# Weighting expert 0's output one expert later, with expert 1 added at a ratio, in an attention-and-experts kernel

## The chip, the cores and the metric

The kernel runs on one core of a Trainium2 chip. The metric is the device time of one execution in microseconds (us), the median over several executions. All executions quoted here were of the fast state, and their granted TensorE clock was 0.986 to 1.0 of full speed. A profile shows a span of its own, about 2 us shorter than the time of the same execution (696.4 us in a run of 698.21 us). Engine names in the profile: PE is TensorE, PEld its weight load, DVE is VectorE, ACT is ScalarE, POOL is GpSimd. SBUF is the core's working memory; PSUM is the memory that PE writes its products to, here in banks that are used again and again.

## The reference

Attention for 4 batches and 8 heads (768 tokens, head size 64), then a mixture of 8 experts over the 3072 tokens, each token weighted for each expert by a matrix `P` that Sinkhorn rounds have balanced. Cut to what matters:

```python
x = attention(q, k, v, ...)              # 3072 tokens x 512
P = np.exp(x @ w_gate - max)             # 3072 x 8
for _ in range(8):                       # Sinkhorn: rows, then columns
    P /= P.sum(1, keepdims=True) + 1e-09
    P /= P.sum(0, keepdims=True) + 1e-09
    P *= N / E
for e in range(8):
    h = np.maximum(x @ w1[e], 0.0)
    out += P[:, e:e + 1] * (h @ w2[e])
```

Every output row is a sum over all experts. Expert 0 can be computed before `P` is known if its result is multiplied by `P[:, 0]` later.

## The kernel before

The kernel does that. Expert 0 is computed while attention and the Sinkhorn rounds run, and its unweighted output goes to `acc` in SBUF. Experts 1 to 7 follow, each in six chunks of 512 tokens. Each product of a chunk is built from seven block products instead of eight (Strassen's scheme): PE does 14 layer-1 groups and 7 layer-2 groups a chunk, VectorE makes the sums of blocks, ScalarE copies partial sums out of PSUM. While PE does layer 1 of one chunk, it does layer 2 of the chunk before, in turns.

`Pne` holds the weights; `acc[c]` is the output of chunk `c`. The weighting of expert 0 was a generator that expert 1's loop advanced four times per chunk:

```python
def weight_first(c):
    for nb in range(4 * c, 4 * c + 4):
        nc.scalar.activation(out=acc_of(nb), in_=acc_of(nb), func=AF.Copy,
                             bias=0.0, scale=Pne[:, nb, 0:1])
        yield
...
def copy(g, name, bank):       # layer 1: a partial sum leaves PSUM, VectorE reads it later
    R[name] = mp.tile([128, 2, 256], F32, tag=f"R{name}", bufs=1, name=f"R{name}")
    nc.scalar.activation(out=R[name], in_=banks[g, bank], func=AF.Copy, bias=0.0, scale=1.0)
...
def add(bank, i, n, by_dma):   # layer 2: add weight * result to acc
    ...
        w = Pne[:, 4 * c + 2 * q + i, e:e + 1]
        if by_dma:             # ScalarE weights into t, a DMA with accumulation adds t to acc
            nc.scalar.activation(out=t[:, q, :], in_=banks[bank][q], func=AF.Copy,
                                 bias=0.0, scale=w)
        else:                  # VectorE adds in place
            nc.vector.scalar_tensor_tensor(out=dst, in0=banks[bank][q], scalar=w, in1=dst,
                                           op0=ALU.mult, op1=ALU.add)
...
if e == 1:
    gens["first"] = weight_first(c)
    gens["x"] = combine_x((c + 1) % NCH)
for slot in range(7):
    go("l1", 2 if n == 0 and slot == 0 else 1)
    ...
    go("l2")
    if slot in (2, 3, 5, 6):
        go("first")
...
with tc.manual_schedule(engines={mybir.EngineType.DVE}):
    ...
```

In this part only VectorE's instructions keep the order of the program. The compiler chooses the order of the others, and puts forward what it takes to be ready (the profile and the run e5 below show the order that results).

The softmax here doesn't subtract the row's maximum and nothing guards it: scores larger than these inputs give would overflow.

## Time and profile before

The time was 698.92 us in three runs.

| what | value | view of the profile |
|---|---|---|
| PE busy | 681.5 of 696.4 us | page, part 1 |
| chain that ended last | 89% PE | page, part 4 |
| ScalarE busy, 176 to 203 us | 26.75 of 27.00 us | table of stretches |
| weightings of `acc` | 24, all between 176.2 and 202.4 us | instructions of one source line |
| PE's period, expert 1's six chunks | 13.89, 12.93, 12.32, 12.33, 12.32, 12.22 us | timeline of PE |

A "period" here is the time from one chunk's first layer-2 group to the next chunk's. The steady value is 12.22 us: 14 layer-1 groups of 0.4365 us and 7 layer-2 groups of 0.873 us, one after the other.

The timeline of PE (columns: start, duration, engine, line, operation and operands) gives the starts of the first three chunks' layer 2:

```profile
182.03 1.04 PE L801 MATMUL l2y<-w_1_2286,hT_0_3295 128*128 128x256 f16 x8
...
195.92 1.04 PE L801 MATMUL l2y<-w_1_2286,hT_1_3369 128*128 128x256 f16 x8
...
208.85 1.04 PE L801 MATMUL l2y<-w_1_2286,hT_2_3548 128*128 128x256 f16 x8
```

The differences are 13.89 and 12.93 us. The list of waits (columns: who waited for whom, us in total, times, longest), cut to PE's waits in this stage, names the cause:

```profile
PE l1y L736 <- ACT R_3482 L745: 1.2, 1, 1.2
PE l1y L736 <- ACT R_3663 L745: 0.4, 1, 0.4
```

In this program PE may not write a PSUM bank again before ScalarE has copied it to an R tile. The timelines show the longer of the two waits, on PE and on ScalarE:

```profile
190.24 0.60 PE L736 MATMUL l1y<-T_1_3324,w_1_2284 128*128 128x256 f16 x4
192.00 0.60 PE L736 MATMUL l1y<-T_1_3324,S_1_3308 128*128 128x256 f16 x4 [1.16 <-ACT R_3482 L745]
```

```profile
187.02 2.00 ACT L659 ACTIVATE acc_81<-acc_81,Pne 128x512 f32<-128x512 f32 x3
188.86 1.38 ACT L659 ACTIVATE acc_82<-acc_82,Pne 128x512 f32<-128x512 f32 x2
190.09 0.89 ACT L815 ACTIVATE add<-l2z,Pne 128x256 f32<-128x256 f32 x2
190.80 0.66 ACT L745 ACTIVATE R_3476<-l1w 128x512 f32<-128x512 f32 x1
191.27 0.67 ACT L745 ACTIVATE R_3482<-l1y 128x512 f32<-128x512 f32 x1
```

L659 is the weighting. Five of them stand in front of the `add`, and the copy that PE needs comes behind it. A little earlier ScalarE's timeline shows the same pattern:

```profile
182.66 0.63 ACT L745 ACTIVATE R_3375<-l1y 128x512 f32<-128x512 f32 x1
183.14 1.98 ACT L659 ACTIVATE acc_80<-acc_80,Pne 128x512 f32<-128x512 f32 x3
184.98 0.63 ACT L745 ACTIVATE R_3399<-l1w 128x512 f32<-128x512 f32 x1
```

`acc_80` belongs to chunk 1, although PE is at layer 2 of chunk 0: the compiler had put the weightings of all six chunks as early as it could. The table of stretches (columns: stretch and length; busy time and instruction count of PE, PEld, DVE, ACT, POOL; PE's clock; DMA share; GB/s) shows no idle time on ScalarE:

```profile
176.00:203.00 27.00, 25.84 (x209) 20.13 (x207) 22.69 (x47) 26.75 (x51) 2.63 (x3) 1.00 0.48 80
```

Here ScalarE's 26.75 us is the number to read, and beside it PE's 25.84 us of 27: PE is idle for over a microsecond.

### The profile page before, as it was taken

The page shows a single profiled execution, that of the slowest core. Times are in us where ns is not written, and L with a number is a line of the kernel's source. Part 1 is how long each engine was busy: PE and PEld are TensorE (multiplying, and loading weights), DVE is VectorE, ACT ScalarE, POOL GpSimd, SP SyncE. Part 2 cuts the span into 40 slices and gives each one's busy share as a digit, 9 for nine tenths or more (in the row PEclk, how much of TensorE's full clock was granted, in tenths as well). Part 3 has the DMA queues.
Part 4 walks back from the last instruction along what each step waited for, and adds up shares of the span by engine and source line. Part 5 has one row for each costly group of instructions (what it writes and reads, how often), then busy time and mean ns, then how long its engine had stood idle before and what let it go on. Part 6 is the DMA issues. An engine that isn't in the chain of part 4 may idle for free.

```text
span 696.4 us, 16662 instructions
## 1 busy us (share of the span) xinstructions
PE 681.5 (98%) x6753; PEld 567.3 (81%) x6753; DVE 574.1 (82%) x1149; ACT 420.0 (60%) x775; POOL 167.1 (24%) x201
## 2 busy tenths in 40 slices
PE   7999999999999999999999999999999999999997
PEld 3666666666688888888888888888888888888885
DVE  7886766657889988898898879888898888988785
ACT  6778776764985555546556554655556555555651
POOL 7555430000021131213212221222212212121210
PEclk9999999999999999999999999999999999999999
DMA  9999990001634386437834593359533954245786
GB/s 178 175 172 152 68 80 3 1 2 22 100 61 78 61 135 108 75 64 121 138 57 76 90 152 68 62 81 154 90 58 64 152 103 77 48 76 110 143 158 152
DMA packets 102974, 65.59 MB, mean 94 GB/s; under 512 B 67056, under 2 KB 83440, under 8 KB 102896
## 3 DMA queue, kind: packets, MB, share of 16 engines
q0 software_dynamic: 93696, 57.17, 66.0%
q1 hardware_dynamic: 7552, 6.30, 3.9%
q8 instruction: 53, 0.87, 0.6%
q10 hardware_dynamic: 1648, 1.05, 0.5%
q14 instruction: 25, 0.20, 0.1%
HBM read 52.45 MB, written 6.29 MB: 84 GB/s over the span
## 4 chain that ended last, share of the span: by engine, by line
PE 89%; ACT 5%; DVE 3%; issue 1%; DMA 1%; ACTq 0%; DVEq 0%
PE l1y L736 20%; PE l2y L801 20%; PE l2w L801 10%; PE l1w L736 10%; PE l1z L736 5%; PE l2z L801 5%; PE l1b L716 1%; DMA ret_u<-in_is_retrieval_dram 1%; DVE acc_80 L818 0%; ACT acc_81 L659 0%; ACT acc_82 L659 0%; ACT add L815 0%; DVE hT_2_3548 L751 0%; PE l_3104 L393 0%; PE l_3170 L393 0%
## 5 line engine op out<-in xcount | busy, mean ns | idle before, releaser
L815 ACT ACTIVATE add<-l2z,Pne 128x256 f32<-128x256 f32 x80 | 33.6, 471 | 93.5 <-PE l2z L801 93.5
L815 ACT ACTIVATE add<-l2w,Pne 128x256 f32<-128x256 f32 x80 | 33.6, 471 | 28.6 <-PE l2w L801 27.8
L815 ACT ACTIVATE add<-l2y,Pne 128x256 f32<-128x256 f32 x80 | 33.7, 472 | 11.0 <-PE l2y L801 10.6
L379 PEld LDWEIGHTS <-w_0_124 128*128 128x128 f16 x384 | 35.5, 98 | 4.2 <-issue 0.4
L823 POOL DMA_DIRECT2D acc_79<-add x21 | 17.7, 845 | 79.1 <-ACT add L815 23.2
L823 POOL DMA_DIRECT2D acc_82<-add x21 | 17.8, 845 | 68.0 <-ACT add L815 31.1
L823 POOL DMA_DIRECT2D acc_81<-add x21 | 17.7, 844 | 67.9 <-ACT add L815 30.2
L823 POOL DMA_DIRECT2D acc_80<-add x21 | 17.7, 845 | 67.7 <-ACT add L815 26.9
L823 POOL DMA_DIRECT2D acc_83<-add x18 | 15.2, 844 | 54.2 <-ACT add L815 23.0
L823 POOL DMA_DIRECT2D acc_84<-add x18 | 15.4, 855 | 43.8 <-ACT add L815 37.7
L736 PEld LDWEIGHTS <-S_3_4656 128*128 128x128 f16 x192 | 18.8, 98 | 2.2
L736 PEld LDWEIGHTS <-S_2_3586 128*128 128x128 f16 x192 | 18.8, 98 | 2.2
L736 PEld LDWEIGHTS <-S_4_5690 128*128 128x128 f16 x192 | 18.8, 98 | 2.2
L736 PEld LDWEIGHTS <-S_7_8792 128*128 128x128 f16 x192 | 18.8, 98 | 2.2
L736 PEld LDWEIGHTS <-S_6_7758 128*128 128x128 f16 x192 | 18.8, 98 | 2.2
L736 PEld LDWEIGHTS <-S_5_6724 128*128 128x128 f16 x192 | 18.8, 98 | 2.2
L818 DVE SCALAR_TENSOR_TENSOR acc_83<-l2y,Pne,acc_83 128x256 f32<-128x256 f32 x44 | 19.2, 477 | 1.3 <-PE l2y L801 1.3
L818 DVE SCALAR_TENSOR_TENSOR acc_80<-l2y,Pne,acc_80 128x256 f32<-128x256 f32 x42 | 18.3, 477 | 1.4 <-PE l2y L801 1.4
L818 DVE SCALAR_TENSOR_TENSOR acc_79<-l2y,Pne,acc_79 128x256 f32<-128x256 f32 x42 | 18.3, 477 | 1.3 <-PE l2y L801 1.3
L818 DVE SCALAR_TENSOR_TENSOR acc_81<-l2y,Pne,acc_81 128x256 f32<-128x256 f32 x42 | 18.3, 477 | 1.3 <-PE l2y L801 1.3
L818 DVE SCALAR_TENSOR_TENSOR acc_82<-l2y,Pne,acc_82 128x256 f32<-128x256 f32 x42 | 18.3, 477 | 1.3 <-PE l2y L801 1.3
L736 PEld LDWEIGHTS <-S_1_3308 128*128 128x128 f16 x160 | 15.6, 98 | 4.2 <-issue 1.9
(2563 smaller groups left out, 2261.8 us busy)
## 6 DMA issues: line engine op xcount, KB each, us to landing
acc_79<-add POOLq DMA_DIRECT2D x21, 256.0 KB, 3.6
acc_80<-add POOLq DMA_DIRECT2D x21, 256.0 KB, 3.3
acc_81<-add POOLq DMA_DIRECT2D x21, 256.0 KB, 3.3
acc_82<-add POOLq DMA_DIRECT2D x21, 256.0 KB, 3.3
acc_83<-add POOLq DMA_DIRECT2D x18, 256.0 KB, 3.5
acc_84<-add POOLq DMA_DIRECT2D x18, 256.0 KB, 10.1
w_0_124<-in_moe_w_dram POOLq DMA_DIRECT2D x1, 1024.0 KB, 11.5
w_0_131<-in_moe_w_dram POOLq DMA_DIRECT2D x1, 1024.0 KB, 18.1
```

The costliest lines, as they stand in the source:

```text
L379: nc.tensor.matmul(out=l1[:, ts(fb % 2, 256)], lhsT=w1[:, dc, ts(fb, 128)], rhs=xT[dc // 2][:, dc % 2, c0:c0 + 256], start=(dc == 0), stop ...
L716: nc.tensor.matmul(out=l1, lhsT=w1[:, dc, ts(fb, 128)], rhs=xT[dc // 2][:, dc % 2, ts(c, CH)], start=(dc == 0), stop=(dc == 3),)
L736: nc.tensor.matmul(out=banks[g, bank][:, f, :], lhsT=lefts1[e][k - 1][:, dc, ts(2 * g + f, 128)], rhs=rights1[c][k - 1][:, dc, :], start=( ...
L801: nc.tensor.matmul(out=banks[bank][q], lhsT=lefts2[e, c][k - 1][:, q, f, :], rhs=rights2[e][k - 1][:, f, :], start=(first and q == 0 and f ...
L815: nc.scalar.activation(out=t[:, q, :], in_=banks[bank][q], func=AF.Copy, bias=0.0, scale=w)
L818: nc.vector.scalar_tensor_tensor(out=dst, in0=banks[bank][q], scalar=w, in1=dst, op0=ALU.mult, op1=ALU.add,)
L823: nc.gpsimd.dma_start(out=acc[c][:, i, n, :, :], in_=t, accum_op=ALU.add)
```

## The change

Its intent: in expert 1, ScalarE should not weight at all. Expert 1 is added to the unweighted expert 0 at the ratio `P1/P0`; then, in expert 2, the whole is multiplied by `P0`, before expert 2 is added to it. To choose the moment, VectorE (whose order is fixed) copies the weights to a small tile `wt` just before ScalarE may use them. One more, unrelated edit joins two loads of each k and q tile into one. The diff, cut to its core:

```diff
-                for c in range(2):
-                    nc.gpsimd.dma_start(out=dst[:, c],
-                                        in_=s.rearrange("h (p c) d -> c p h d", c=2)[c])
+                nc.gpsimd.dma_start(out=dst, in_=s.rearrange("h (p c) d -> p c h d", c=2))
 ...
+    LATE = 2
+    over0 = xp.tile([128, NB, LATE], F32, tag="over0")
 ...
+    def weigh_over():
+        nc.vector.reciprocal(out=over0[:, :, 0], in_=Pne[:, :, 0])
+        nc.vector.tensor_tensor(
+            out=over0[:, :, 1:], in0=Pne[:, :, 1:LATE],
+            in1=over0[:, :, 0:1].broadcast_to([128, NB, LATE - 1]), op=ALU.mult)
+
+    def weight_of(e, nb):
+        return (over0 if e < LATE else Pne)[:, nb, e:e + 1]
+
     def weight_first(c):
-        for nb in range(4 * c, 4 * c + 4):
-            nc.scalar.activation(out=acc_of(nb), in_=acc_of(nb), func=AF.Copy,
-                                 bias=0.0, scale=Pne[:, nb, 0:1])
-            yield
+        wt = mp.tile([128, 4], F32, tag="wt", name=f"wt_{c}")
+        def hold(i0, i1):
+            nc.vector.tensor_copy(out=wt[:, i0:i1], in_=Pne[:, 4 * c + i0:4 * c + i1, 0])
+        def weigh(i0, i1):
+            for i in range(i0, i1):
+                x = acc_of(4 * c + i)
+                nc.scalar.activation(out=x, in_=x, func=AF.Copy, bias=0.0, scale=wt[:, i:i + 1])
+        hold(0, 1)
+        yield
+        weigh(0, 1)
+        yield
+        hold(1, 4)
+        yield
+        weigh(1, 4)
+        yield
 ...
-                w = Pne[:, 4 * c + 2 * q + i, e:e + 1]
+                w = weight_of(e, 4 * c + 2 * q + i)
 ...
+        if e == LATE:
+            gens["first"] = weight_first(c)
         if e == 1:
-            gens["first"] = weight_first(c)
             gens["x"] = combine_x((c + 1) % NCH)
         for slot in range(7):
+            if slot in (1, 2):
+                go("first")
             go("l1", 2 if n == 0 and slot == 0 else 1)
+            if slot in (1, 2):
+                go("first")
 ...
-            if slot in (2, 3, 5, 6):
-                go("first")
 ...
             if n == 0 and slot == 0:
                 run(combine_w(1), 9)
+                weigh_over()
```

## The prediction

> **What bounds the kernel.** TensorE. The page gives PE 681.5 of 696.4 us busy, and the chain that ended last is 89% PE. From about 222 us to the tail the table of stretches shows no PE idle. So a change without matmul changes can win at most PE's 15 us of idle: about 6 in the first 40 us, about 5 at the end, under 1 per 40 us in attention, about 1.8 recorded from 160 to 200.
>
> **Where this change can act.** Expert 1's first two chunks. There the timeline shows 24 weightings of `acc` (128x512, about 0.61 us each back to back, near 14.7 us in all) from 176.3 to 202.4 between ReLUs and PSUM copies, and ScalarE without idle from 176 to 203. It is late with copies that free a bank: the list of PE's waits has l1y behind R copies, 1.2 and 0.4 us. PE's period for one chunk (14 layer-1 and 7 layer-2 groups) is 13.89, then 12.93 us; expert 1's next chunks take 12.3, expert 2's 12.23. Work alone is 14 x 0.4365 + 7 x 0.873 = 12.22. The remaining 0.1 of expert 1's other chunks is not ScalarE's: VectorE is 98% busy there (12.0 of 12.3).
>
> **What the change does.** The order of PE's instructions is identical. The 24 weightings leave expert 1 and appear as 1 + 3 per chunk of expert 2, on weights that VectorE copies at its place in its order (12 tiny copies, about 0.1 us each, an estimate). VectorE gets a reciprocal and a product of 128x24 (0.30 us measured for the same reciprocal; about 0.5 together) where it idles 2.03 us (180.8 to 182.8) for ScalarE's last ReLU. Those ReLUs are then no longer delayed, so VectorE's first sum can start about 0.9 us earlier (estimate).
>
> In expert 2, ScalarE is busy 6.9 of 12.25 us per chunk, with gaps of 0.92, 0.60 and 2.46 us. The first weighting (0.61) falls in the 0.60 gap, the three others (about 1.85) in the 2.46 gap before the l2z copy. VectorE is at 11.1 of 12.25: two copies fit. I expect no PE wait.
>
> The merged loads of k and q: 18 fewer software DMAs of 0.88 us of POOL each, 16 us less POOL. PE's waits name no load after the start: worth 0 (plus or minus 0.3 us).
>
> **Sum.** 13.89 + 12.93 fall to about 2 x 12.33: 2.16 us saved, all on the critical path because PE is saturated afterwards. 698.9 - 2.2 = **696.7 us**, range 695.8 to 698.2. Faster by over 2%: 0.01; within 2%: 0.985; slower by over 2%: 0.005. The Trainium skill, "Perfetto Trace Analysis" (Optimization Strategy), suggests interleaving regimes whose most-contended engine differs; this trace agrees, but only 2 us were there to win.
>
> **What would show it.** Right: ScalarE idle again from 176 to 203; no l1y wait on R copies in the first two chunks; periods 12.3, 12.3; expert 2's period still 12.23 with ScalarE near 9.3; POOL busy about 151; PE idle of 0 to 160 as before. Wrong: first-chunk periods above 12.6 (then VectorE, not ScalarE, was the limit); expert 2's periods above 12.3; new waits of transposes on loads.
>
> **What would make it wrong.** VectorE at 98% in expert 1 may keep PE waiting with ScalarE free. The three weightings may delay the l2z copy (up to 0.3 us x 6). Larger DMAs may land later than needed, or earlier loads may shorten attention (0.5 us).

## The result and the profile after

The changed kernel took 696.43 us (695.75 to 697.29, six runs) against 698.8 us (698.18 to 698.95, six runs). The ratio is 0.9967, with a 95% interval of 0.9955 to 0.998. Ratios in this document are the mean time of one kernel's fast runs over that of the other's of the same rounds, so they are not quite the ratio of the medians. The gain of 2.4 us is small but clear of the noise.

The same three lines of PE's timeline:

```profile
182.11 1.04 PE L827 MATMUL l2y<-w_1_2268,hT_0_3278 128*128 128x256 f16 x8
...
194.34 1.04 PE L827 MATMUL l2y<-w_1_2268,hT_1_3350 128*128 128x256 f16 x8
...
206.57 1.03 PE L827 MATMUL l2y<-w_1_2268,hT_2_3525 128*128 128x256 f16 x8
```

Both periods are now 12.23 us. The third chunk starts 2.28 us earlier than before (206.57 against 208.85), although the first started 0.08 us later. The profile's span fell by 2.4 us (696.4 to 694.0), so what was won here was kept to the end.

ScalarE's timeline around the same place no longer holds a weighting, and it waits for PE (the bracket is the idle time before an instruction, and what ended it):

```profile
183.62 0.60 ACT L771 ACTIVATE R_3380<-l1w 128x512 f32<-128x512 f32 x1 [1.09 <-PE l1w L762]
184.12 0.59 ACT L771 ACTIVATE R_3386<-l1y 128x512 f32<-128x512 f32 x1
185.37 0.60 ACT L771 ACTIVATE R_3407<-l1y 128x512 f32<-128x512 f32 x1 [0.66 <-PE l1y L762]
```

The stretch from 176 to 203 us: ScalarE is busy for 15.44 us instead of 26.75, PE for the whole 27. The `add` and the two copies that came at 190.09, 190.80 and 191.27 us now start at 188.43, 189.16 and 189.75.

```profile
176.00:203.00 27.00, 27.00 (x226) 21.85 (x224) 25.44 (x54) 15.44 (x31) 3.49 (x4) 1.00 0.47 81
```

In the list of PE's waits the two lines with R copies are gone. And the weightings' new place, in expert 2's second chunk:

```profile
257.85 0.59 ACT L771 ACTIVATE R_4454<-l1y 128x512 f32<-128x512 f32 x1
258.32 0.72 ACT L678 ACTIVATE acc_80<-acc_80,wt_4441 128x512 f32<-128x512 f32 x1
259.10 0.60 ACT L771 ACTIVATE R_4474<-l1y 128x512 f32<-128x512 f32 x1
259.59 1.95 ACT L678 ACTIVATE acc_80<-acc_80,wt_4441 128x512 f32<-128x512 f32 x3
262.10 0.84 ACT L841 ACTIVATE add<-l2z,Pne 128x256 f32<-128x256 f32 x2 [0.56 <-PE l2z L827]
```

The copy of `l2z` still waits for PE, by 0.56 us: the three weightings in front of it were done in time. The same gap was 2.46 us without them. Expert 2's periods are 12.22 and 12.23 us, as before.

A measure with less noise than the time helps below: in a profile, the stretch from the first layer-2 group of expert 1 to the 41st chunk's, the last that is done in seven products. It leaves out the start of the kernel, where profiles of kernels with the same code there differed by up to 0.9 us (the first layer-2 group came at 181.90 us in e9, at 182.79 in e2). It was 491.81 us before and 489.38 after: 2.43 us less, of which the first two periods are 13.89 + 12.93 - 2 x 12.23 = 2.36; one odd period of 12.31 us late in the profile of before is most of the rest.

### The profile page after: what moved, and what is told of

Its sections match the earlier page's. It is cut to its first block, busy times and chain, and to the rows that moved or that the text cites. A ratio compares the mean times of both kernels' runs of the same rounds, so it can differ in the third digit from the quotient of the medians.

```text
span 694.0 us, 16657 instructions
## 1 busy us (share of the span) xinstructions
PE 680.4 (98%) x6753; PEld 567.4 (82%) x6753; DVE 575.5 (83%) x1163; ACT 422.0 (61%) x775; POOL 158.0 (23%) x183
## 4 chain that ended last, share of the span: by engine, by line
PE 92%; ACT 3%; DVE 3%; issue 1%; POOL 0%; DVEq 0%; ACTq 0%
PE l1y L762 21%; PE l2y L827 21%; PE l1w L762 10%; PE l2w L827 10%; PE l2z L827 5%; PE l1z L762 5%; PE l1b L742 1%; PE l_3153 L391 0%; PE l_3087 L391 0%; PE l_1496 L391 0%; ACT PT_1_0_0_302 L479 0%; PE l_3069 L391 0%; PE last_10519 L879 0%; PE last_10507 L879 0%; PE l_3229 L391 0%
## 5 line engine op out<-in xcount | busy, mean ns | idle before, releaser
L841 ACT ACTIVATE add<-l2z,Pne 128x256 f32<-128x256 f32 x68 | 28.5, 470 | 74.1 <-PE l2z L827 74.1
L841 ACT ACTIVATE add<-l2w,Pne 128x256 f32<-128x256 f32 x68 | 28.5, 470 | 24.4 <-PE l2w L827 23.6
L841 ACT ACTIVATE add<-l2y,Pne 128x256 f32<-128x256 f32 x68 | 28.5, 470 | 10.6 <-PE l2y L827 8.9
L844 DVE SCALAR_TENSOR_TENSOR acc_83<-l2y,Pne,acc_83 128x256 f32<-128x256 f32 x38 | 16.6, 478 | 1.3 <-PE l2y L827 1.3
L844 DVE SCALAR_TENSOR_TENSOR acc_79<-l2y,Pne,acc_79 128x256 f32<-128x256 f32 x36 | 15.7, 478 | 1.3 <-PE l2y L827 1.3
L844 DVE SCALAR_TENSOR_TENSOR acc_80<-l2y,Pne,acc_80 128x256 f32<-128x256 f32 x36 | 15.7, 478 | 1.3 <-PE l2y L827 1.3
L844 DVE SCALAR_TENSOR_TENSOR acc_82<-l2y,Pne,acc_82 128x256 f32<-128x256 f32 x36 | 15.7, 478 | 1.3 <-PE l2y L827 1.3
L844 DVE SCALAR_TENSOR_TENSOR acc_81<-l2y,Pne,acc_81 128x256 f32<-128x256 f32 x36 | 15.7, 478 | 1.3 <-PE l2y L827 1.3
```

## The experiments

All kernels of one group shared runs of the kernel before on the same chip; its medians were 698.93 (e1 to e4), 698.84 (e5 to e7) and 698.91 us (e8, e9); the row of the changed kernel is from its own rounds, whose before had 698.8 us. Summary, with the stretch just defined:

| kernel | time, us (range, runs) | ratio to before (95%) | stretch, us |
|---|---|---|---|
| before | 698.93 (698.17 to 699.4, 9) | 1 | 491.81 |
| after | 696.43 (695.75 to 697.29, 6) | 0.9967 (0.9955 to 0.998) | 489.38 |
| e1: merged loads alone | 699.04 (698.36 to 699.7, 5) | 1.0002 (0.9989 to 1.0014) | 491.78 |
| e2: late weighting alone | 696.43 (695.76 to 696.8, 5) | 0.9965 (0.9952 to 0.9977) | 489.38 |
| e3: before, no weighting | 696.43 (695.76 to 697.07, 5) | 0.9966 (0.9954 to 0.9979) | 489.46 |
| e4: held back, in expert 1 | 698.58 (697.55 to 699.02, 5) | 0.9993 (0.998 to 1.0007) | see below |
| e5: late, not held back | 715.37 (714.21 to 715.93, 4) | 1.0235 (1.0221 to 1.0249) | 507.79 |
| e6: late, twice the passes | 702.14 (701.67 to 702.33, 4) | 1.0047 (1.0034 to 1.0061) | 495.27 |
| e7: after, no weighting | 696.58 (695.84 to 696.62, 5) | 0.9964 (0.9951 to 0.9978) | 489.57 |
| e8: two R buffers | 696.59 (695.57 to 696.87, 5) | 0.9965 (0.9953 to 0.9978) | 489.28 |
| e9: chunk 0 alone late | 697.0 (696.24 to 697.55, 5) | 0.9973 (0.9959 to 0.9987) | 489.97 |

### e1 and e2: the two halves of the change

e1 is the kernel before with only the loads edit:

```diff
-                for c in range(2):
-                    nc.gpsimd.dma_start(out=dst[:, c],
-                                        in_=s.rearrange("h (p c) d -> c p h d", c=2)[c])
+                nc.gpsimd.dma_start(out=dst, in_=s.rearrange("h (p c) d -> p c h d", c=2))
```

> The kernel before with the loads of k and q merged and nothing else. Theory (ScalarE's backlog in expert 1 was the cost): same as before, 698.8 us within 0.3; PE's first two chunk periods of expert 1 stay 13.9 and 12.9 us; POOL's busy time falls by about 9 us from 0 to 120 us of the span as it did in the changed kernel. Rival (the gain came from 18 fewer software DMAs): about 696.4 us, and the start of expert 1 comes 2 us earlier.

e2 is the changed kernel with that edit undone.

> The changed kernel with the loads of k and q in two pieces again. Theory: the whole gain stays, 696.4 us within 0.4, periods of the first two chunks 12.2 and 12.2 us. Rival (merged loads): 698.8 us.

e1 took 699.04 us, e2 696.43 us. The merged loads are worth nothing that can be measured; the whole gain is the late weighting. e1's first two periods are 13.91 and 12.95 us, e2's 12.22 and 12.23. POOL lost 9.1 us of busy time with the merged loads (167.1 to 158.0 in the changed kernel, also 158.0 in e1). In the kernel before no engine waited for these loads; in the changed kernel one weight load of PE waited 0.2 us for a merged one. The Trainium skill, "DMA: Bandwidth & Descriptors" (Rules for kernel authors), advises coalescing many small transfers; these pieces were 128 KB each, and joining them moved no time here. A merged load took longer to land (median 13.2 us in the changed kernel, 8.1 for a piece before).

### e3: was it the weightings, or VectorE?

VectorE was busy for 98% of expert 1's later chunks, so it was a rival cause. e3 deletes the weightings from the kernel before and moves nothing (its result is wrong):

```diff
-            nc.scalar.activation(out=acc_of(nb), in_=acc_of(nb), func=AF.Copy,
-                                 bias=0.0, scale=Pne[:, nb, 0:1])
             yield
```

> Wrong result on purpose: the kernel before with its 24 weightings by expert 0 deleted, nothing put in their place. Theory: they alone made ScalarE late, so this is as fast as the changed kernel, 696.4 us within 0.4, first two periods 12.2 to 12.3 us. Rival (VectorE, 98% busy in expert 1, was the limit there, and the changed kernel gains by its other order): periods of the first two chunks stay above 12.6 us, time 697.5 us or more.

It took 696.43 us, with periods of 12.23 and 12.23 us: as fast as the changed kernel. The 24 weightings cost the 2.4 us; VectorE's load, which e3 leaves as it was, did not by itself.

### e7: do they cost anything where they stand now?

e7 deletes them from the changed kernel (wrong result), and leaves VectorE's copies:

```diff
-                nc.scalar.activation(out=x, in_=x, func=AF.Copy, bias=0.0, scale=wt[:, i:i + 1])
+                pass
```

> Wrong result on purpose: the changed kernel without the 24 weightings in expert 2 (the copies on VectorE stay). Theory (they are free where they stand now): the time of the changed kernel within 0.3, 696.3 us; expert 2's periods 12.23 us in both. Rival (they still cost something there): 1 us less or more.

696.58 us, and a stretch of 489.57 us against 489.38 with them (one period of 12.43 us late in e7's profile, far from this code, makes the difference). The six periods with weightings are 12.22 or 12.23 us in both kernels. So no cost of the weightings can be measured in expert 2.

### e6: how much room is there?

Each weighting is followed by a second pass at weight 1.0, so that each chunk of expert 2 has eight passes instead of four:

```diff
                 nc.scalar.activation(out=x, in_=x, func=AF.Copy, bias=0.0, scale=wt[:, i:i + 1])
+                nc.scalar.activation(out=x, in_=x, func=AF.Copy, bias=0.0, scale=1.0)
```

> The changed kernel with each weighting followed by a second pass over the same data at weight 1.0 (result unchanged): 24 more passes of 0.61 us on ScalarE in expert 2. Theory (expert 2's gaps of 0.60 and 2.46 us hold four passes but not eight): the l2z copy comes about 1.8 us late, PE waits for R copies in expert 2, about 0.5 to 1.5 us per chunk, 699 to 705 us. Rival (ScalarE has room for anything in expert 2, since it is only 77% busy there): 696.4 us within 0.5.

702.14 us: the six periods in which PE does layer 1 of expert 2's chunks are 13.21 us each (the first of them is the sixth of the table above, in which layer 2 is still expert 1's). That is 0.98 us more than 12.23, together 5.9 us, which is the whole loss (stretch 495.27 - 489.38 = 5.89). PE's waits in this stretch are those of the kernel before again, only smaller and in every chunk:

```profile
PE l1y L763 <- ACT R L772: 4.1, 6, 0.7
```

That is 0.68 of the 0.98 us of each period. The compiler also changed PE's order in this kernel (in each of the six periods three of eight matmuls of an `l2w` group stand in front of the `l1y` group that waits), so the 0.98 us is not a clean price for four passes. Still, four passes left PE without a wait and eight did not, although ScalarE's mean load in the second chunk of expert 2 (9.31 of 12.23 us, 76%) seemed to leave 2.9 us for the 2.4 us of four more.

### e5: is holding them back needed?

The weightings take `Pne` itself, and VectorE copies nothing:

```diff
-        wt = mp.tile([128, 4], F32, tag="wt", name=f"wt_{c}")
 ...
-            nc.vector.tensor_copy(out=wt[:, i0:i1], in_=Pne[:, 4 * c + i0:4 * c + i1, 0])
+            pass
 ...
-                nc.scalar.activation(out=x, in_=x, func=AF.Copy, bias=0.0, scale=wt[:, i:i + 1])
+                nc.scalar.activation(out=x, in_=x, func=AF.Copy, bias=0.0,
+                                     scale=Pne[:, 4 * c + i, 0:1])
```

> The changed kernel, but the weightings take Pne itself: no copies on VectorE, nothing holds them back. By the order of instructions they then stand on ScalarE already in expert 1's chunks 1 to 5 (and the last four in expert 2), each first one right behind the additions by DMA to the same chunk, and wait for those to land. Theory (the copies' place in VectorE's order is needed): ScalarE stalls 1 to 2 us per chunk on DMA landings and PE loses 1 us or more per chunk, 700 to 706 us. Rival (only the distance from expert 1's first chunk matters): 696.4 us within 0.4.

715.37 us: 19 us worse than the changed kernel, and beyond the expected range. The direction was as the theory had it, the size was not. Without the copies nothing but the data decides when a weighting is ready, and the compiler moved each chunk's four weightings forward by four chunks, right behind expert 1's additions by DMA to the same chunk. (The expectation said that only the last four would remain in expert 2's chunks; by the trace it is the last eight.) ScalarE's timeline has nothing else in between: it stands still until the additions land (list of ScalarE's waits, 182 to 275 us; a seventh wait, of 6.88 us, ends at 276.93):

```profile
ACT acc L677 <- DMA acc<-add: 12.9, 6, 5.9
```

The first seven periods are 12.23, 13.72, 13.33, 13.39, 13.42, 19.14 and 19.08 us. Four of them lose the 1.1 to 1.5 us that the expectation spoke of. The two that lose 6.9 us each are what it left out. In both, a load of the next expert's weights (1 MB) was issued just ahead of the addition (at 247.52 and at 265.18 us), and ScalarE waited for the addition behind it. POOL's timeline and ScalarE's show the first:

```profile
247.52 1.09 POOL L151 DMA_DIRECT2D w<-in_moe_w_dram  x1
248.73 0.83 POOL L849 DMA_DIRECT2D acc<-add  x1
```

```profile
259.08 1.33 ACT L677 ACTIVATE acc<-acc,Pne 128x512 f32<-128x512 f32 x2 [5.91 <-DMA acc<-add]
```

From the issue to the end of ScalarE's wait is 10.35 us (259.08 - 248.73), and 10.85 the second time; the median addition of e5 landed in 3.3 us. The Trainium skill, "DMA: Bandwidth & Descriptors" (Issuing engines are not separate DMA queues), says that transfers run on the same 16 DMA engines and interleave, whichever engine issued them. The 10.35 against 3.3 us agrees with that, but no run moved the load away, so the load as the cause of the long landing is argued from the trace and not shown. What e5 shows is that without the twelve tiny copies on VectorE (about 0.15 us each) the change loses 19 us.

### e4 and e9: is the ratio needed, or is spreading enough?

The rival to the ratio is plain spreading: leave the weightings in expert 1 with plain weights, but hold them back, four per chunk. e4 does this (with loads in two pieces; e2 is its base):

```diff
-        return (over0 if e < LATE else Pne)[:, nb, e:e + 1]
+        return Pne[:, nb, e:e + 1]
 ...
-        if e == LATE:
+        if e == 1:
             gens["first"] = weight_first(c)
 ...
-                weigh_over()
```

> The weightings stay in expert 1 with plain weights (no ratio), but four per chunk, held back by VectorE's copies as in the changed kernel; loads in two pieces. Theory (there is no room in expert 1's first chunk, where the weighting has to come before VectorE's first addition): the first chunk still loses 1 to 2 us and the second nothing; 697.3 to 698.2 us. Rival (only the burst of 24 in a row was harmful, so spreading them is enough and the ratio is not needed): 696.4 us within 0.4, all periods 12.2 to 12.3 us.

698.58 us, a little above the range expected by the theory and 2.15 us above e2. The four weightings of chunk 0 stand among its ReLUs (ScalarE's timeline), and VectorE's first sum waits for the last of these:

```profile
180.37 2.81 ACT L680 ACTIVATE acc<-acc,wt 128x512 f32<-128x512 f32 x4
183.09 1.55 ACT L748 ACTIVATE hT<-l1b 128x512 f16<-128x512 f32 x3
```

```profile
184.67 0.69 DVE L701 TENSOR_TENSOR S<-hT 128x1024 f16<-128x1024 f16 x1 [2.80 <-ACT hT L748]
```

From the first layer-1 group after the plain chunk to the third chunk's layer 2, e4 took 26.95 us (182.07 to 209.02), the changed kernel 25.33 (181.24 to 206.57), the kernel before 27.70 (181.15 to 208.85). So e4 lost 1.62 us in this place, and its next three periods were 12.46 instead of 12.33 us, another 0.39. But the compiler had also exchanged some PE groups in e4, so what the weightings and what the other order cost could not be told apart. e9 goes further: it differs from e4 only in chunk 0, which takes the ratio and is weighted in expert 2, and its PE order is that of the changed kernel.

```diff
-        return Pne[:, nb, e:e + 1]
+        return (over0 if e == 1 and nb < 4 else Pne)[:, nb, e:e + 1]
 ...
-        if e == 1:
+        if (e, c) == (2, 0) or (e == 1 and c > 0):
             gens["first"] = weight_first(c)
 ...
                 run(combine_w(1), 9)
+                weigh_over()
```

> As e4 (weightings in expert 1, four per chunk, held back by VectorE's copies), except chunk 0: that one takes the ratio in expert 1 and is weighted in expert 2. The order of PE's instructions is that of the changed kernel, which it was not in e4. Theory (what e4 lost was mostly chunk 0's weighting among its ReLUs; the rest is VectorE's two copies per chunk, 0.13 us a chunk): first two periods 12.2 to 12.4 us, the next three about 12.4 to 12.5, time 0.3 to 0.8 us over the changed kernel, 696.7 to 697.2 us. Rival (weightings anywhere in expert 1 cost it): first two periods 13 us or more, 698.5 us.

697.0 us; periods 12.33, 12.34, 12.46, 12.45, 12.46. The sum of what is over the changed kernel's periods is 0.59 us, which is what the stretch shows (489.97 - 489.38). So of the gain over before, most needs only spreading plus an exception for chunk 0; having nothing to weight or hold in expert 1 is worth the last 0.6 us (by the profiles; the intervals of the two times overlap). Chunk 0 is where plain spreading failed: its weighting has to come before VectorE's first addition and so, on ScalarE, among the ReLUs. How much of e4's loss in chunk 0 is the weighting itself and how much the PE order that came with it stays open, since e9 takes away both.

### e8: the last tenth in expert 1

Three chunks of expert 1 have periods of 12.32 or 12.33 us before and after. The prediction put that down to VectorE's load. e8 gives the R tiles a second buffer:

```diff
-            R[name] = mp.tile([128, 2, 256], F32, tag=f"R{name}", bufs=1, name=f"R{name}")
+            R[name] = mp.tile([128, 2, 256], F32, tag=f"R{name}", bufs=2, name=f"R{name}")
```

> The changed kernel with two buffers instead of one for each R tile (ScalarE's copies of the PSUM sums, which VectorE's ReLU-sums read). It asks what the last 0.1 us per chunk in expert 1's chunks 3 to 5 is. Theory A (ScalarE's copy waits for VectorE to have read the old R, because there is one buffer): those periods fall from 12.33 to 12.23 us, time 0.3 us under the changed kernel, about 696.1 us, hard to see in the times. Theory B (the prediction's: VectorE is 98% busy there and simply late, whatever the buffers): periods stay 12.33 us, time 696.4 us.

All periods of expert 1 are then 12.22 or 12.23 us: theory A. In the changed kernel, ScalarE's timeline has the two copies at a distance of 0.84 us after the start of the `add`, and 0.60 us between them:

```profile
212.88 0.84 ACT L841 ACTIVATE add<-l2z,over_3012 128x256 f32<-128x256 f32 x2 [2.46 <-PE l2z L827]
213.72 0.60 ACT L771 ACTIVATE R_3809<-l1w 128x512 f32<-128x512 f32 x1
214.32 0.60 ACT L771 ACTIVATE R_3815<-l1y 128x512 f32<-128x512 f32 x1
```

VectorE's timeline has the two instructions that read the old R tiles; they end at 213.61 and 214.20 us, each about 0.1 us before the copy into the same tile starts:

```profile
212.92 0.69 DVE L777 CUSTOM_DVE_ANT_0 hT_3_3703<-l1y,R_3733 128x512 f16<-128x512 f32 x1
213.52 0.68 DVE L777 CUSTOM_DVE_ANT_0 hT_3_3703<-l1w,R_3739 128x512 f16<-128x512 f32 x1
```

In e8, where the copy goes to the other buffer, the copies follow more closely, at 0.73 and 0.47 us:

```profile
212.85 0.84 ACT L841 ACTIVATE add<-l2z,over 128x256 f32<-128x256 f32 x2 [2.45 <-PE l2z L827]
213.58 0.60 ACT L771 ACTIVATE R<-l1w 128x512 f32<-128x512 f32 x1
214.05 0.61 ACT L771 ACTIVATE R<-l1y 128x512 f32<-128x512 f32 x1
```

PE's second `l1y` group here starts 0.54 us after the one before it in the changed kernel (first pair), and 0.43 us in e8 (second pair):

```profile
214.43 0.60 PE L762 MATMUL l1y<-T_3_3565,w_1_2266 128*128 128x256 f16 x4
214.97 0.60 PE L762 MATMUL l1y<-T_3_3565,S_1_3291 128*128 128x256 f16 x4
```

```profile
214.35 0.60 PE L762 MATMUL l1y<-T,w 128*128 128x256 f16 x4
214.78 0.60 PE L762 MATMUL l1y<-T,S 128*128 128x256 f16 x4
```

VectorE is as busy in both (12.04 us in such a period), but with two buffers its lateness no longer reaches ScalarE's copies. The Trainium skill, "Perfetto Trace Analysis" (Optimization Strategy), says that the same gap repeating on an engine that should be saturated can mean too few buffers; this trace agrees, with 0.1 us in each of three chunks. The five periods together are 0.31 us shorter. The times do not resolve this (696.59 against 696.43 us, in different rounds), and e8's profile has one odd period of 12.44 us elsewhere. So e8 is not shown to be faster than the changed kernel.

## Why the prediction was right

- **The time.** 696.7 us was predicted, with 695.8 to 698.2 as the range; 696.43 us was measured. The class, within 2%, was right too.
- **What was to be won.** The prediction found PE saturated everywhere but in a few places, and 2.2 us lost in expert 1's first two chunks. e3 shows that removing the weightings by itself wins 2.4 us, and e7 that no more is won by removing them altogether.
- **The step that was mis-sized.** "13.89 + 12.93 fall to about 2 x 12.33" was too cautious: they fell to 2 x 12.23. The prediction took the 0.1 us of the later chunks as a property of all chunks of expert 1. In the changed kernel VectorE has 11.71 and 11.81 us of work in the first two periods and 12.04 in the next three, which fits the extra 0.1 us of these; no run varied that work. Predicted 2.16, measured 2.36 us.
- **The reason given for that 0.1 us** ("VectorE is 98% busy there") was only half of it: it was the single R buffer that handed VectorE's lateness on to ScalarE and PE (e8). A high busy share did not by itself cost PE anything.
- **Expert 2's gaps.** The first weighting was to fall in the 0.60 us gap and three in the 2.46 us gap. They did: the copy after the first came 0.06 us later relative to the chunk (counted from ScalarE's first copy of the chunk: 259.10 - 255.84 = 3.26, before 261.30 - 258.10 = 3.20 us), and the `l2z` copy not at all (6.26 us both times). ScalarE's busy time is 9.31 us of the period, as predicted (9.3).
- **VectorE's first sum** was to start about 0.9 us earlier; it started at 182.07 instead of 182.84 us, 0.77 us earlier, or 0.85 us if the later start of the stage (0.08) is counted.
- **The merged loads** were predicted to be worth nothing, and e1 shows that. POOL's saving was mis-sized: 16 us were predicted (18 DMAs of 0.88 us), 9.1 measured, because one merged load takes POOL 1.23 to 1.37 us, not 0.88.
- **What the prediction did not see** is how much depends on VectorE's copies. It took the place of the weightings from the changed kernel's order and never asked what they would do without those copies. e5 answers that: 19 us worse.

Still open: what four further passes cost in expert 2 without the change of PE's order (e6); how much of the 2.36 us came through the late R copies and how much through VectorE's first sum, which also started late (e3 and the change mend both at once); and whether two R buffers are faster in the time (e8).

## What to carry to other kernels

When an engine that is idle 40% of the time still delays the busiest one, look for a burst: work that became ready all at once and that the scheduler put in front of short, urgent copies. Here moving it to a later stage cost nothing measurable, because each piece fitted a gap that the timeline shows; e6 suggests that the gaps, not the mean load, say how much fits. Where the scheduler orders by readiness, make the work become ready at the right moment, for example by an input that an engine with a fixed order writes; otherwise a freed dependency can bring it forward behind a slow transfer and stall the engine.

## What the Trainium skill lacked or had wrong

- "ScalarE: Activation LUTs" (What ACT_TABLE_LOAD costs) gives an ACTIVATE as 186 ns + 0.833 ns per element + about 93 ns for a pointer operand, with about 93 ns of overlap between neighbours. For 512 elements that is an estimate of 706 ns and a distance of 613 ns. The weightings took 705 to 724 ns in expert 2 and followed each other at about 0.61 us, so the page is right here. In the kernel before, amid the burst, the same instruction is recorded with 710 to 808 ns, but the pace stayed at 0.61 us (three in the 1.84 us from 183.14 to 184.98). We found no page that says what stretches the record, and no run here shows it.
- "DMA: Bandwidth & Descriptors" (Anatomy of one DMA) fits a DMA from GpSimd as 2.0 us plus bytes over 436e3, an estimate of 2.6 us for the 256 KB of an accumulating SBUF-to-SBUF transfer. Here such a transfer landed after 3.3 us (median for most chunks), and after 10.1 us (median) in the chunk where 1 MB loads had been issued around it. The formula has no term for accumulation or for a transfer ahead of it; which of them makes up the difference is not shown here.
- The same page calls the cost of descriptor generation small and variable. That row gives no figure. One load in two pieces took POOL about 0.88 us for each, and 1.23 to 1.37 us in one piece: twice the data cost 0.35 to 0.49 us more in one instruction.
- No page draws the conclusion for scheduling on which this change turns: an instruction that is put forward while its input still comes by DMA stalls everything behind it on its engine, and a tiny copy on another engine can hold it back. In e5 the absence of these copies cost 19 us.
